# Adding a partial product into the residual ahead of its eviction, in a fused attention and MLP kernel on one Trainium2 core

## The chip, the core and the metric

The kernel runs on one core of a Trainium2 chip. The metric is the device time of one launch in microseconds (us). The core has a matrix engine (TensorE, PE in the profile; its weight loads are PEld), a vector engine (VectorE, DVE), an activation engine (ScalarE, ACT), a general engine (GpSimd, POOL) and a queue engine that issues transfers (SyncE, SP). Each works through its own instructions in order; between engines, semaphores say when a value is there or a buffer is free. TensorE writes its results to PSUM, whose banks VectorE and ScalarE read; GpSimd works on SBUF.

## The reference

A linear attention with decay, followed by a normalised two-layer MLP with a residual:

```
for b in range(nb):                       # blocks of 64 rows of each sequence
    intra = einsum('bhic,bhjc->bhij', qb, kb) * Dmask
    intra = einsum('bhij,bhjd->bhid', intra, vb)
    inter = einsum('bhid,bhde->bhie', qb * lam_pow, kv_state)
    out[:, :, sl] = intra + inter
    kv_state = lam_block * kv_state + einsum('bhsd,bhse->bhde', kb * rev_pow, vb)
x  = out as [4, 768, 512]
xn = (x - mean) / sqrt(var + 1e-6) * g_ln
result = x + relu(xn @ w_ch1) @ w_ch2     # w_ch1 512 x 2048, w_ch2 2048 x 512
```

q, k and v are 4 x 8 x 768 x 64 in float32; the result is 4 x 768 x 512 in float32.

## The kernel before, in words

The 3,072 rows of the result are worked in twelve units of 256 rows (u = 0 to 11, `NU` is 12). A unit is two tiles of 128 rows, called ab = 0 and ab = 1. For each unit the attention part leaves a tile `x` of 128 partitions x 2 x 512 (the residual; four buffers) and, transposed, the normalised input `xT` of the MLP. The scale of the normalisation, `rstd`, is put on at the very end, one value per row. A group of the MLP is one unit: g = u.

The first MLP layer (`m1`, line 502) runs 64 matmuls per group into eight PSUM tiles `pm`, and ScalarE puts each tile through a ReLU into `hT`. The order of all work is written out by hand (lines 1009 to 1284): `units(n)` issues the next n pieces of the MLP, and between them stand the attention steps of the unit ahead, the stores and the loads. Instructions of each engine run in the order in which these lines issue them.

For groups 0 to 5 the second layer is the plain product (`m2`, line 624). For groups 6 to 11 (`WG = 6`) it is a scheme with seven products in place of eight, by Strassen's method, over the two tiles of rows and the two halves of the 512 output columns. `h_sums` (line 520) forms sums of parts of `hT` on VectorE, and sums of the weights (`wt`) are made once. `m2w` (line 599) issues the products P1, P2, P7, P6, P5, P4, P3 in this order, eight matmuls of 256 columns each, spread over eight pieces of seven matmuls. There are four accumulators `pr["a"]` to `pr["d"]` (pwa to pwd in the profile), each 128 x 256 in a bank of its own:

- a takes P1, and then P6 on top of it
- b takes P2
- c takes P7, and then P4 on top of it
- d takes P5, and is then begun anew with P3

All four come from the ring of four `mm` tiles that `pm` uses too, so each has to be read before the ring comes round to it.

As soon as a product is complete, `evict` (line 550) reads it out. `scaled` (line 557) is one VectorE operation: accumulator x rstd + a third operand. `o` is the output tile, 128 x 2 x 512, and `oq[ab][z]` its quarters of 256 columns, as `xq` are those of x. Before the change, an eviction does the following:

- P1: ScalarE reads a x rstd into `ev_u1` (line 569), GpSimd adds x and writes the first quarter (570)
- P2: VectorE adds b into the first quarter
- P7: ScalarE reads c x rstd into `ev_p7` (577)
- P6: VectorE makes quarter (0, 1) from a and x (579)
- P5: VectorE adds d into `ev_p7` (581), makes both quarters of tile 1 from a and x in one operation of 512 columns (582), and GpSimd adds `ev_p7` into quarter (1, 1) (584)
- P4: VectorE adds c into quarter (1, 0) (586)
- P3: VectorE adds d into quarter (0, 1) (591)

The second product in a bank can only begin once the first has been read where its value is needed alone: P6 after ScalarE's read of P1, P4 after ScalarE's read of P7, P3 after VectorE's read of P5.

A group's output is stored by `store(u)` (line 671), two transfers on SP's queue, issued later in the hand-written order. The last group (u = 11) is stored from within `evict` instead: quarter (0, 0) after P2 (line 575, two transfers on SP), all of tile 1 after P4 (line 589, one transfer on SP and one on ScalarE's queue), and quarter (0, 1) after P3 (line 594, one on each).

Of the kernel before, what the change touches and what calls it, by code (L numbers as in the profile page):

```python
# [11 lines left out]
ALU = mybir.AluOpType  # L12
# [5 lines left out]
def kernel(  # L18
# [11 lines left out]
    nc = tc.nc  # L30
# [4 lines left out]
    NU = B * S // W  # L35
    DM = H * D
# [20 lines left out]
    half = [slice(0, 64), slice(64, 128)]  # L57
# [434 lines left out]
    o_of = {}  # L492
    m2s = {}

    def mlp(g):
# [36 lines left out]
        pr = {}  # L532
# [15 lines left out]
        ev = {}  # L548

        def evict(i):  # L550
            u = g
            x, rstd = x_keep[u]
            w = DM // 2
            r = [rstd[:, ab:ab + 1] for ab in range(2)]
            xq = [[x[:, ab, z * w:(z + 1) * w] for z in range(2)] for ab in range(2)]

            def scaled(out, in0, ab, in1):
                nc.vector.scalar_tensor_tensor(out, in0=in0, scalar=r[ab], in1=in1, op0=ALU.mult, op1=ALU.add)  # L558

            def tmp(name):  # L560
                ev[name] = wk.tile([128, w], F32, tag="ev_" + name, bufs=1, name="ev_" + name)
                return ev[name]

            if i == "P1":
                o_of[u] = wk.tile([128, 2, DM], F32, tag="o", bufs=2, name="o")
            o = o_of[u]
            oq = [[o[:, ab, z * w:(z + 1) * w] for z in range(2)] for ab in range(2)]
            if i == "P1":
                nc.scalar.activation(tmp("u1"), pr["a"], ACT.Identity, scale=r[0])  # L569
                nc.gpsimd.tensor_tensor(oq[0][0], ev["u1"], xq[0][0], op=ALU.add)  # L570
            elif i == "P2":
                scaled(oq[0][0], pr["b"], 0, oq[0][0])
                if u == NU - 1:
                    for j in range(2):
                        nc.sync.dma_start(rows_of(u)[j][:, 0, 0:w], o[half[j], 0, 0:w])
            elif i == "P7":
                nc.scalar.activation(tmp("p7"), pr["c"], ACT.Identity, scale=r[1])
            elif i == "P6":
                scaled(oq[0][1], pr["a"], 0, xq[0][1])
            elif i == "P5":  # L580
                scaled(ev["p7"], pr["d"], 1, ev["p7"])
                scaled(o[:, 1].rearrange("p (z w) -> p z w", z=2), pr["a"][:, None, :].to_broadcast([128, 2, w]), 1,
                       x[:, 1].rearrange("p (z w) -> p z w", z=2))
                nc.gpsimd.tensor_tensor(oq[1][1], ev["p7"], oq[1][1], op=ALU.add)  # L584
            elif i == "P4":
                scaled(oq[1][0], pr["c"], 1, oq[1][0])
                if u == NU - 1:
                    for j in range(2):
                        (nc.sync, nc.scalar)[j].dma_start(rows_of(u)[j][:, 1], o[half[j], 1])
            elif i == "P3":  # L590
                scaled(oq[0][1], pr["d"], 0, oq[0][1])
                for j in range(2):
                    if u == NU - 1:
                        (nc.sync, nc.scalar)[j].dma_start(rows_of(u)[j][:, 0, w:], o[half[j], 0, w:])

        products = (("P1", "a", True), ("P2", "b", True), ("P7", "c", True), ("P6", "a", False),
                    ("P5", "d", True), ("P4", "c", False), ("P3", "d", False))
# [1 line left out]
        def m2w(n):  # L599
            lo, hi = 7 * n, 7 * n + 7  # L600
            for q, (i, bank, first) in enumerate(products):
                part = [r for r in range(8) if lo <= 8 * q + r < hi]
                if part:
                    product(i, bank, part, first and part[0] == 0)
                    if part[-1] == 7:
                        evict(i)
# [44 lines left out]
    def rows_of(u):  # L651

        cc, b = divmod(u, B)
        order = "(c p j) d -> j p c d" if u < LB else "(j c p) d -> j p c d"
        return out[b, cc * W:(cc + 1) * W, :].rearrange(order, c=2, j=2)
# [658 lines left out]
```

## Time and profile before

| what | value |
|---|---|
| median of 6 runs | 214.7 us (213.0 to 216.69) |
| the profiled execution | 213.78 us |
| its span, first to last instruction | 212.1 us |
| granted TensorE clock, mean | 0.999 |
| GpSimd's add of P7 (line 584), six times | 726 ns each |
| ScalarE's read of P7 (line 577), six times | 476 ns each |
| VectorE's evictions of 256 columns, of 512 columns | 471 to 484 ns, 743 ns |

The profile is of one execution. The span is shorter than the execution's own time, since it runs from the first to the last instruction only. A row of the timeline has the start in us from the span's start, the duration in us, the engine, the line and the operation, with what it writes and what it reads, and in brackets how long the engine was idle before it and what ended that idle time. A row of the waits has the waiting engine and line, what it waited for, the total in us, how often, and the longest. SPq and ACTq are the queues on which a transfer is issued; such a row is the time of the issue, not of the transfer. Matmuls overlap: a row of eight matmuls begins with the first one and ends with the last, and the next product's row begins before that.

### The profile page before, as it was taken

The page shows a single profiled execution, that of the slowest core. Times are in us where ns is not written, and L with a number is a line of the kernel's source. Part 1 is how long each engine was busy: PE and PEld are TensorE (multiplying, and loading weights), DVE is VectorE, ACT ScalarE, POOL GpSimd, SP SyncE. Part 2 cuts the span into 40 slices and gives each one's busy share as a digit, 9 for nine tenths or more (in the row PEclk, how much of TensorE's full clock was granted, in tenths as well). Part 3 has the DMA queues.
Part 4 walks back from the last instruction along what each step waited for, and adds up shares of the span by engine and source line. Part 5 has one row for each costly group of instructions (what it writes and reads, how often), then busy time and mean ns, then how long its engine had stood idle before and what let it go on. Part 6 is the DMA issues. An engine that isn't in the chain of part 4 may idle for free.

```text
span 212.1 us, 7030 instructions
## 1 busy us (share of the span) xinstructions
PE 199.3 (94%) x3027; PEld 150.8 (71%) x3027; DVE 141.2 (67%) x292; ACT 97.8 (46%) x195; POOL 83.1 (39%) x113
## 2 busy tenths in 40 slices
PE   1989999999999999999999899999999999999991
PEld 0379788544784675685586488888888888988880
DVE  2587570559268437737986589798897887875271
ACT  2854869220452244355093085285383471652620
POOL 4559138239565181228073064182381302011011
PEclk9999999999999999999999999999999999999999
DMA  3999999999999999899899999999995330520312
GB/s 92 295 275 217 188 295 188 203 303 268 221 305 221 195 223 200 175 238 140 162 216 204 138 241 197 203 212 182 208 195 100 82 73 0 124 29 8 94 25 74
DMA packets 94144, 37.15 MB, mean 175 GB/s; under 512 B 68385, under 2 KB 91169, under 8 KB 94114
## 3 DMA queue, kind: packets, MB, share of 16 engines
q1 hardware_dynamic: 89584, 32.32, 70.3%
q0 software_dynamic: 4224, 4.19, 12.6%
q8 instruction: 23, 0.38, 0.8%
q10 hardware_dynamic: 306, 0.20, 0.3%
q14 instruction: 7, 0.06, 0.1%
HBM read 27.27 MB, written 6.29 MB: 158 GB/s over the span
## 4 chain that ended last, share of the span: by engine, by line
PE 75%; DVE 7%; DMA 6%; ACT 4%; POOL 3%; issue 2%; SPq 1%; ACTq 0%; DVEq 0%
PE pm L510 35%; PE pm L641 10%; PE pwa L545 5%; PE pwd L545 5%; PE pwc L545 5%; DMA kqT<-kq 4%; PE pwb L545 2%; PE pm1t L615 2%; PE po L418 2%; DMA g_one<-in_moe_g_ln_dram 2%; PE tp L249 2%; PE po L431 2%; PE sc L272 2%; DVE xc L460 1%; POOL kq L235 1%
## 5 line engine op out<-in xcount | busy, mean ns | idle before, releaser
L510 PE MATMUL pm<-xT,w 128*128 128x256 bf16 x736 | 85.4, 273 | 0.4 <-issue 0.3
L510 PEld LDWEIGHTS <-w 128*128 128x128 bf16 x736 | 69.9, 98 | 10.6 <-issue 1.3
L513 ACT ACTIVATE hT<-pm 128x512 f16<-128x512 f32 x92 | 55.1, 603 | 41.1 <-PE pm L510 40.3
L641 PE MATMUL pm<-w,hT 128*128 128x512 f16 x192 | 43.3, 379 | 0.0
L641 PEld LDWEIGHTS <-hT 128*128 128x128 f16 x192 | 18.2, 98 | 20.6
L312 POOL TENSOR_TENSOR Sn<-Stmp,lam_s 128x256 bf16<-128x256 f32 x16 | 9.8, 613 | 47.5 <-DVE Stmp L390 26.7
L545 PEld LDWEIGHTS <-hs 128*128 128x128 f16 x192 | 18.8, 98 | 2.2
L460 DVE SCALAR_TENSOR_TENSOR xc<-po,mv,g_row 128x512 bf16<-128x512 f32 (+1 forms) x24 | 16.8, 706 | 1.8
L282 DVE TENSOR_TENSOR mA<-sc,keep 128x512 bf16<-128x512 f32 x20 | 13.1, 685 | 7.2 <-PE sc L272 7.1
L453 ACT COPY x<-po 128x512 f32<-128x512 f32 x18 | 9.9, 590 | 16.8 <-PE po L431 10.7
L570 POOL TENSOR_TENSOR o<-ev_u,x 128x256 f32<-128x256 f32 x6 | 4.6, 771 | 30.7 <-ACT ev_u L569 30.7
L545 PEld LDWEIGHTS <-hT 128*128 128x128 f16 x144 | 13.6, 98 | 2.7 <-ACT hT L513 1.2
L455 DVE BATCH_NORM_STATS2 stats<-x 128x6 f32<-128x512 f32 x18 | 12.4, 688 | 3.8 <-ACT x L453 3.8
L528 DVE TENSOR_TENSOR hs<-hT 128x1024 f16<-128x1024 f16 x12 | 9.6, 801 | 7.1 <-ACT hT L513 7.1
L665 DVE SCALAR_TENSOR_TENSOR o<-pm,rstd,x 128x512 f32<-128x512 f32 x12 | 8.8, 744 | 6.9 <-PE pm L641 6.8
L235 POOL TENSOR_TENSOR kq<-qin,lam_q 128x512 bf16<-128x512 f32 x10 | 10.3, 1045 | 6.3 <-DMA qin<-in_q_dram 3.8
L241 POOL TENSOR_TENSOR vb<-vin,lam_p 128x1024 bf16<-128x1024 f32 x6 | 11.4, 1896 | 3.5 <-DMA vin<-in_v_dram 3.5
L235 POOL TENSOR_TENSOR kq<-qin,lam_p 128x512 bf16<-128x512 f32 x12 | 12.3, 1042 | 0.4 <-DMA qin<-in_q_dram 0.4
L241 POOL TENSOR_TENSOR vb<-vin,lam_v 128x1024 bf16<-128x1024 f32 (+1 forms) x7 | 11.6, 1661 | 2.2 <-DMA vin<-in_v_dram 1.1
L584 POOL TENSOR_TENSOR o<-ev_p,o 128x256 f32<-128x256 f32 x6 | 4.4, 726 | 20.5 <-DVE o L558 20.5
L358 DVE TENSOR_TENSOR mA<-sc,keep 128x512 bf16<-128x512 f32 x12 | 8.2, 683 | 2.0 <-PE sc L352 2.0
L558 DVE SCALAR_TENSOR_TENSOR o<-pwa,rstd,x 128x256 f32<-128x256 f32 (+1 forms) x12 | 7.4, 613 | 3.0 <-PE pwa L545 3.0
(124 smaller groups left out, 260.1 us busy)
## 6 DMA issues: line engine op xcount, KB each, us to landing
out_dram<-o SPq DMA_DIRECT2D x22, 256.0 KB, 4.3
w<-in_moe_w_ch_dram POOLq DMA_DIRECT2D x8, 512.0 KB, 8.7
kin<-in_k_dram SPq DMA_DIRECT2D x14, 256.0 KB, 4.1
qin<-in_q_dram SPq DMA_DIRECT2D x14, 256.0 KB, 4.7
vin<-in_v_dram SPq DMA_DIRECT2D x14, 256.0 KB, 5.5
kin<-in_k_dram SPq DMA_DIRECT2D x5, 512.0 KB, 6.8
qin<-in_q_dram SPq DMA_DIRECT2D x5, 512.0 KB, 8.7
vin<-in_v_dram SPq DMA_DIRECT2D x5, 512.0 KB, 8.2
```

The source lines that it names most:

```text
L235: eng.tensor_tensor(part(1, st[u]["kq"], ALL)[:, :, :, j], src[:, :, :, j], lq[:, :, :, None].to_broadcast([128, NP, 2, D]), op=ALU.mult)
L241: eng.tensor_tensor(st[u]["vb"][:, hs], qkv_in[u]["v"][:, hs], lv.to_broadcast([128, n, 2, D]), op=ALU.mult)
L282: nc.vector.tensor_tensor(s[f"mA{hf}"][:, e], s[f"sc{hf}"][e], kp[:, None, :, :].to_broadcast([128, 2, 2, 128]), op=ALU.mult)
L312: eng.tensor_tensor(dst, src, lam_s[:, :, None].to_broadcast([128, NP, D]), op=ALU.mult)
L453: nc.scalar.copy(x, po)
L455: nc.vector.bn_stats(stats, po if early else x)
L460: nc.vector.scalar_tensor_tensor(xc[:, sl], in0=po[:, sl], scalar=mv[:, 0:1], in1=g_row[:, sl], op0=ALU.subtract, op1=ALU.mult)
L510: nc.tensor.matmul(pm[:, b, :], lhsT=w1[n // W2K][:, kk, (n % W2K) * 128:(n % W2K + 1) * 128], rhs=xT_of[g][:, kk, 0:N], start=(b == 0 and ...
L513: nc.scalar.activation(hT[:, u * NB:(u + 1) * NB, 0:N], pm, ACT.Relu)
L528: nc.vector.tensor_tensor(s13, b[:, :, 1:2, :].to_broadcast([128, n, 2, 128]), b[:, :, 0:4:3, :], op=ALU.subtract)
L545: nc.tensor.matmul(pr[bank], lhsT=lhs(r), rhs=rhs, start=(first and r == 0), stop=(r == KB // 2 - 1), skip_group_check=True)
L641: nc.tensor.matmul(acc[i], lhsT=hT[:, kk, i * 128:(i + 1) * 128], rhs=w2[kk // W2K][:, kk % W2K, :], start=(kk == 0), stop=(kk == KB - 1))
```

## The change

At P7, GpSimd adds ScalarE's read-out into x itself (quarter (1, 1) of x), at once. P6's eviction makes both quarters of tile 1 from a and x, in one operation of 512 columns; x already has P7 in it there. P5's eviction adds d into quarter (1, 1) of the output and then makes quarter (0, 1) from a and x. GpSimd's add after P5 goes. In the last group the quarters of tile 1 are stored one by one, each as it becomes complete (after P5 and after P4), through a helper that issues one transfer on SP's queue and one on ScalarE's.

```diff
             elif i == "P7":
                 nc.scalar.activation(tmp("p7"), pr["c"], ACT.Identity, scale=r[1])
+                nc.gpsimd.tensor_tensor(xq[1][1], ev["p7"], xq[1][1], op=ALU.add)
             elif i == "P6":
-                scaled(oq[0][1], pr["a"], 0, xq[0][1])
-            elif i == "P5":
-                scaled(ev["p7"], pr["d"], 1, ev["p7"])
                 scaled(o[:, 1].rearrange("p (z w) -> p z w", z=2), pr["a"][:, None, :].to_broadcast([128, 2, w]), 1,
                        x[:, 1].rearrange("p (z w) -> p z w", z=2))
-                nc.gpsimd.tensor_tensor(oq[1][1], ev["p7"], oq[1][1], op=ALU.add)
+            elif i == "P5":
+                scaled(oq[1][1], pr["d"], 1, oq[1][1])
+                scaled(oq[0][1], pr["a"], 0, xq[0][1])
+                last_rows(1, 1)
             elif i == "P4":
                 scaled(oq[1][0], pr["c"], 1, oq[1][0])
-                if u == NU - 1:
-                    for j in range(2):
-                        (nc.sync, nc.scalar)[j].dma_start(rows_of(u)[j][:, 1], o[half[j], 1])
+                last_rows(1, 0)
             elif i == "P3":
                 scaled(oq[0][1], pr["d"], 0, oq[0][1])
-                for j in range(2):
-                    if u == NU - 1:
-                        (nc.sync, nc.scalar)[j].dma_start(rows_of(u)[j][:, 0, w:], o[half[j], 0, w:])
+                last_rows(0, 1)
+
+        def last_rows(ab, z):
+            u = g
+            if u < NU - 1:
+                return
+            sl = slice(z * (DM // 2), (z + 1) * (DM // 2))
+            for j, eng in enumerate((nc.sync, nc.scalar)):
+                eng.dma_start(rows_of(u)[j][:, ab, sl], o_of[u][half[j], ab, sl])
```

## The prediction

> **What bounds the kernel now.** I read four views: the page's totals, the waits of TensorE from 122 us on (where the groups with seven products run), the timeline of one such group, and the timeline of the end.
>
> ```profile
> PE 199.3 (94%) x3027; PEld 150.8 (71%) x3027; DVE 141.2 (67%) x292; ACT 97.8 (46%) x195; POOL 83.1 (39%) x113
> PEclk9999999999999999999999999999999999999999
> ```
>
> ```profile
> PE sc L352 <- DMA kqT<-kq: 1.0, 1, 1.0
> PE pm L510 <- issue: 0.3, 1, 0.3
> ```
>
> These two are all of TensorE's waits from 122 to 206 us, the DMA one at 122 us, before the first product (129.5 us). From there TensorE is never idle and at full clock. Idle time put in front of it is added to the end; work taken off another engine gains nothing. Now the third of the six groups (start, duration, engine, line):
>
> ```profile
> 161.16 1.04 PE L545 MATMUL pwc<-wt,hs 128*128 128x256 f16 x8
> 162.03 1.04 PE L545 MATMUL pwa<-wt,hs 128*128 128x256 f16 x8
> 162.29 0.48 ACT L577 ACTIVATE ev_p<-pwc,rstd 128x256 f32<-128x256 f32 x1 [1.27 <-PE pwc L545]
> 162.91 1.04 PE L545 MATMUL pwd<-wt,hs 128*128 128x256 f16 x8
> 163.11 0.48 DVE L558 SCALAR_TENSOR_TENSOR o<-pwa,rstd,x 128x256 f32<-128x256 f32 x1 [0.55 <-PE pwa L545]
> 163.78 1.04 PE L545 MATMUL pwc<-wt,hT 128*128 128x256 f16 x8
> 164.05 0.48 DVE L558 SCALAR_TENSOR_TENSOR ev_p<-pwd,rstd,ev_p 128x256 f32<-128x256 f32 x1 [0.46 <-PE pwd L545]
> 164.45 0.74 DVE L558 SCALAR_TENSOR_TENSOR o<-pwa,rstd,x 128x512 f32<-128x512 f32 x1
> 164.65 1.04 PE L545 MATMUL pwd<-w,hs 128*128 128x256 f16 x8
> 165.27 0.72 POOL L584 TENSOR_TENSOR o<-ev_p,o 128x256 f32<-128x256 f32 x1 [3.39 <-DVE o L558]
> 165.30 0.48 DVE L558 SCALAR_TENSOR_TENSOR o<-pwc,rstd,o 128x256 f32<-128x256 f32 x1
> ```
>
> TensorE begins a product every 0.87 us: P7 at 161.16, P6 162.03, P5 162.91, P4 163.78, P3 164.65. P3 overwrites bank d, so it must wait until P5's value there is read. That read (DVE, 164.05) ends at 164.53, 0.12 us before P3. This is the narrowest place. VectorE idles 0.55 us before P6's eviction and 0.46 us before P5's.
>
> **What doesn't change.** Per group VectorE keeps six operations and 1,792 columns (before 256+256+256+512+256+256, after 256+512+256+256+256+256), ScalarE its two reads, GpSimd two adds. "P5's eviction is one operation" frees bank d no earlier: d's read was already the first of P5's two operations. The removed add L584 (0.73 us) released nobody on TensorE: the stores of groups 6 to 10 wait for P3's eviction, which ends later (166.21 against 165.99). Gain there: nothing. Bank a, read last by P5's second operation in both kernels, is wanted after P3 only.
>
> **What is added: GpSimd in the chain to P3.** P6's eviction, now 512 wide, reads the quarter of x that GpSimd just wrote; P5's eviction reads what P6's wrote; VectorE works in order, and P3 waits for it. GpSimd is free: L570 ended at 161.88. From the end of P7's read, 162.29 + 0.476 = 162.77:
> - to GpSimd's start 0.085 (P1's read ended 161.015, L570 began 161.10);
> - the add 0.726 (L584; L570, with the same kind of operands, took 726 to 788 ns, the upper value where a VectorE operation with two SBUF operands was already running, which is not so here);
> - to VectorE 0.06: the Smid that follows a GpSimd Sn started 0.04 after its end (168.11, 168.15), and this operation waits for two engines, as P5's eviction does, which began 0.10 after its last matmul (163.95, 164.05), so 0.04 to 0.10;
> - the 512-wide operation 0.743, from PSUM, as in L558's long form;
> - to the dependent operation 0.11: P4's eviction at 165.30 began so long after the 512-wide one ended (165.19), with the same two waits (own engine and TensorE); other dependent VectorE pairs show 0.03 to 0.04;
> - P5's read of d 0.484;
> - to TensorE 0.06: the first transpose of xc began 0.05 after its VectorE operation (29.60, 29.65).
>
> Sum 2.27 us. Today's schedule gives from that read's end to P3 164.65 − 162.77 = 1.88 us. TensorE therefore stands 2.27 − 1.88 = 0.39 us before P3. In the first group the read ends at 132.92 and P3 begins at 134.85: 1.93, stall 0.34; the other five have 1.88 or 1.89. With every link at its lower value (0.08, 0.72, 0.04, 0.74, 0.03, 0.47, 0.05 = 2.13) the stall is 0.25, with every upper one (0.09, 0.79, 0.10, 0.75, 0.11, 0.49, 0.06 = 2.39) 0.51.
>
> Behind the waiting P6 operation VectorE has only P5's, P4's and P3's evictions; P4's begins no later than now. Behind the stalled P3 on TensorE lies all later work, and nothing there waits for anything else that could swallow the delay. The 0.1 us between P3's last matmul and the next 64x64 matmul recurs at changes of matmul shape all through the kernel, so I don't count it as cover.
>
> Two rules bear on this. The Trainium skill, VectorE: DVE Perf Modes, section on the TRN2 errata, prices an operation from PSUM at 120 cycles plus its columns at 0.96 GHz: 658 and 392 ns, 1.05 us for the pair. The rows say 0.743 + 0.484 = 1.23. With the page's prices the stall is 0.21 us, with the rows' 0.39. I take the rows. And Perfetto Trace Analysis, "Optimizing Scalar/DVE Operations", says that larger operations pay where the engine is saturated, but where it is not and holds others up, smaller ones let work finish sooner. VectorE is at 67%: the rule speaks against putting the wide operation ahead of the one TensorE waits for. As two halves, the one without GpSimd first, the chain would hold 0.484 in place of 0.743 and the stall would be 0.13. The change doesn't do that.
>
> **The end.** In the last group:
>
> ```profile
> 207.41 0.48 DVE L558 SCALAR_TENSOR_TENSOR o<-pwd,rstd,o 128x256 f32<-128x256 f32 x1
> 207.71 0.47 SPq L589 DMA_DIRECT2D out_dram<-o  x1
> 207.71 0.54 ACTq L589 DMA_DIRECT2D out_dram<-o  x1
> 208.27 0.55 SPq L594 DMA_DIRECT2D out_dram<-o  x1
> 208.35 0.75 ACTq L594 DMA_DIRECT2D out_dram<-o  x1
> ```
>
> The second half of o waits for GpSimd's add (206.96 + 0.72 = 207.68) and is issued at 207.71; P3's quarter, ready at 207.89, queues behind that issue until 208.27 and 208.35. It lands 2.3 and 2.5 us later, at 210.85 at the latest; the span ends 1.25 after that. Changed, still without the earlier groups' delay: P5's read ends at 206.28 + 0.39 = 206.67, its stores go at 206.7; P4's eviction ends near 207.47, its stores take the queues from 207.5 to 208.05; P3's eviction is at 207.41 + 0.39 = 207.80, done 208.28, stores at 208.32. So the queueing that goes pays for the last stall: the last issue is where it was, with 64 KB instead of 128 KB per queue just ahead. Landing after 2.0 us (this group's first 64 KB stores, alone) to 2.5: a gain of 0 to 0.5, I take 0.3. The two added issues, one on each queue, fit into gaps.
>
> **Sum.** Five earlier groups 0.34 + 4 × 0.39 = 1.90, less 0.3: +1.6 us. The profiled execution took 213.78 (span 212.1 and 1.7 around it): 215.4. The median of the runs is 214.7: 216.3, which I predict. The bounds give 5 × 0.25 − 0.5 = +0.75 and 5 × 0.51 = +2.55.
>
> **Rivals.**
> - *The stall at P3*, as above: 216.3, 75%. For it: 0.12 us of room against an operation that starts 0.5 us later and is 0.26 longer. Own range 215.3 to 217.4.
> - *The chain fits* (the side not slower): if it takes under 1.88 us, P3 doesn't wait and only the end moves: P3's quarter, ready at 207.89, would be issued behind P4's at 208.1 and land 0.2 earlier by that and up to 0.5 by the smaller load, −0.5 in all: 214.2. It decides below 1.88, which needs 0.39 us off my sum; even the lower values total 2.13. A stall of 0.1 gives 5 × 0.1 − 0.3 = +0.2, 214.9. Together 16%.
> - *The chain is longer*, GpSimd's add slowed and each hand-over at its upper value: 5 × 0.51 = +2.55, 217.25, 7%.
> - *Faster by over 0.5%*: there is no idle TensorE time to recover and the end offers 0.7 us at most, 0.3%. Only scatter: 2%.
>
> Half a per cent, 1.1 us, is about what a measurement of this kernel can tell from no change. Of the main case some 2 points fall below it, so slower is 0.80, same 0.18, faster 0.02. The range 214.4 to 218.0 takes in the bounds and the scatter of the median (runs from 213.0 to 216.69).
>
> **What would show it.** P6's eviction waiting for GpSimd's x and starting 0.5 us later; P3's first matmul 2.2 to 2.3 us after the end of P7's read; a new TensorE wait on VectorE, some 0.4 us, six times; the last stores issued with nothing queued before them, landing in under 2.5. P2's stores and the order of all operations stay as they are. Wrong if P3 follows P4 without a gap, or if TensorE's later waits shrink by as much.

## The result and the profile after

The changed kernel takes 216.66 us (median of 33 runs) against 214.59 us for the kernel before (70 runs on the same chips): ratio 1.0106, interval 1.0087 to 1.0125, slower by 1.9 to 2.7 us. The ratios leave out executions more than 1.5% above the fastest of their kernel (the profiles of e1 and e6 below are such, so their first starts are not used), a limit that one fast run moves; over all runs the two means are 1.8 us apart. Later runs of it gave 1.0085 (1.0052 to 1.0118) and 1.0123 (1.0086 to 1.0160). The kernel before, run against itself, gave 0.9969 (0.9939 to 0.9999) and 0.9971 (0.9931 to 1.0011): a single comparison can be off by 0.3%. The forecast was 216.3.

The profiled execution took 216.43, its span 214.73 (212.06 before). The totals of the page, busy us of each engine:

```profile
PE 200.7 (93%) x3027; PEld 150.7 (70%) x3027; DVE 140.0 (65%) x292; ACT 98.2 (46%) x195; POOL 83.8 (39%) x113
PEclk9999999999999999999999999999999999999999
```

As many matmuls, at the same clock. The totals do not say where the time went: TensorE's busy time grew by 1.4 of the 2.7 us by which the span grew, since the ends of its matmuls are modelled and part of a short wait counts as work. TensorE's waits from 122 us to the end:

```profile
PE pm L510 <- issue: 1.2, 2, 0.9
PE pwd L545 <- DVE o L558: 0.9, 5, 0.2
PE sc L352 <- DMA kqT<-kq: 0.2, 1, 0.2
```

The middle line is new: P3 waits for VectorE's eviction. (Waits under some size aren't listed, here the first of the six, and the view counts from the modelled end of the matmuls before, so the starts of the products measure the wait better.) And among VectorE's waits in the same stretch:

```profile
DVE o L558 <- POOL x L578: 5.6, 6, 1.1
```

That is P6's eviction waiting for GpSimd's add, six times. The third group's timeline, which answers to the one shown of before:

```profile
163.37 1.04 PE L545 MATMUL pwc<-wt,hs 128*128 128x256 f16 x8
164.50 0.48 ACT L577 ACTIVATE ev_p<-pwc,rstd 128x256 f32<-128x256 f32 x1 [1.27 <-PE pwc L545]
165.05 0.72 POOL L578 TENSOR_TENSOR x<-ev_p,x 128x256 f32<-128x256 f32 x1 [0.97 <-ACT ev_p L577]
165.11 1.04 PE L545 MATMUL pwd<-wt,hs 128*128 128x256 f16 x8
165.81 0.75 DVE L558 SCALAR_TENSOR_TENSOR o<-pwa,rstd,x 128x512 f32<-128x512 f32 x1 [1.05 <-POOL x L578]
165.99 1.04 PE L545 MATMUL pwc<-wt,hT 128*128 128x256 f16 x8
166.67 0.48 DVE L558 SCALAR_TENSOR_TENSOR o<-pwd,rstd,o 128x256 f32<-128x256 f32 x1
167.07 0.48 DVE L558 SCALAR_TENSOR_TENSOR o<-pwa,rstd,x 128x256 f32<-128x256 f32 x1
167.20 1.03 PE L545 MATMUL pwd<-w,hs 128*128 128x256 f16 x8 [0.18 <-DVE o L558]
```

Read it along the diagonal: ScalarE's read of P7 ends at 164.98, GpSimd 165.05 to 165.77, the wide eviction 165.81 to 166.56, the read of bank d 166.67 to 167.15, P3 at 167.20. P3 begins 1.21 us after P4 (165.99), where before it was 0.87: 0.34 us lost on TensorE. The end of the last group:

```profile
207.50 1.14 SPq L575 DMA_DIRECT2D out_dram<-o  x2
209.89 2.08 SPq L599 DMA_DIRECT2D out_dram<-o  x3
209.90 2.18 ACTq L599 DMA_DIRECT2D out_dram<-o  x3
210.99 0.48 DVE L558 SCALAR_TENSOR_TENSOR o<-pwd,rstd,o 128x256 f32<-128x256 f32 x1 [0.34 <-PE pwd L545]
```

The three stores of each queue begin at 209.9, and the last of them at 211.50; 3.23 us later the span ends (214.73). Before it was 3.71 us from the last issue (208.35) to the end (212.06). The 64 KB stores on ScalarE's queue, first before, then after, with the median time from issue to landing last:

```profile
out_dram<-o ACTq DMA_DIRECT2D x1, 64.0 KB, 2.5
out_dram<-o ACTq DMA_DIRECT2D x3, 64.0 KB, 2.2
```

Since TensorE sets the pace, the starts of P1 in the six groups (6 to 11) measure the stages. All profiles of this study, in us, from the traces to 0.001 us and then rounded ("P3 − P4" is the distance of the first matmuls, first group / others; 0.87 is no stall):

| kernel | first P1 at | 6 to 7 | 7 to 8 | 8 to 9 | 9 to 10 | 10 to 11 | last P1 to end | P3 − P4 |
|---|---|---|---|---|---|---|---|---|
| before | 129.51 | 15.01 | 14.79 | 14.54 | 13.95 | 13.20 | 11.05 | 0.87 / 0.87 |
| before, second (e7) | 127.94 | 15.04 | 14.54 | 14.54 | 13.94 | 13.20 | 11.05 | 0.87 / 0.87 |
| before, third (e10) | 129.28 | 15.29 | 14.77 | 14.54 | 13.95 | 13.20 | 11.05 | 0.87 / 0.87 |
| after | 130.25 | 15.93 | 15.33 | 14.88 | 14.29 | 13.54 | 10.50 | 1.16 / 1.22 |
| after, second (e8) | 131.21 | 15.43 | 15.01 | 14.88 | 14.28 | 13.54 | 10.50 | 1.16 / 1.22 |
| after, third (e11) | 130.03 | 15.88 | 15.32 | 14.87 | 14.28 | 13.54 | 10.50 | 1.16 / 1.22 |
| e1, new in the last group only | 132.50 | 15.46 | 14.54 | 14.54 | 13.94 | 13.20 | 10.50 | 0.87; last 1.22 |
| e2, new in the other five only | 131.14 | 15.97 | 15.06 | 14.88 | 14.28 | 13.53 | 11.06 | 1.16 / 1.22; last 0.87 |
| e3, P7 added by VectorE | 131.87 | 15.61 | 15.02 | 15.00 | 13.95 | 13.20 | 10.15 | 1.01 / 0.87; third 1.07 |
| e4, GpSimd twice | 130.59 | 15.76 | 15.34 | 15.34 | 14.74 | 14.00 | 10.97 | 1.62 / 1.68 |
| e5, wide eviction in halves | 129.59 | 15.80 | 14.80 | 14.62 | 14.02 | 13.28 | 10.26 | 0.89 / 0.95 |
| e6, bank d first | 131.70 | 15.68 | 14.60 | 14.54 | 13.94 | 13.20 | 10.29 | 0.87 / 0.87 |
| e6 again (e12) | 129.37 | 15.54 | 14.86 | 14.54 | 13.95 | 13.20 | 10.32 | 0.87 / 0.87 |
| e9, smaller stores only | 130.74 | 15.04 | 14.82 | 14.54 | 13.95 | 13.20 | 11.05 | 0.87 / 0.87 |

The three columns from 8 to 11 and the end repeat to 0.01 us. There the change costs 0.34 us per group, as much as the distance of P3 from P4 grew (1.215 − 0.873): nothing later takes the stall back. Five stalls are 0.29 + 4 × 0.345 = 1.67 us; the last stage, its own stall included, is 0.55 shorter. Together +1.12 us. The median grew by 2.1, the mean over all runs by 1.8. The rest is spoken of below.

### The profile page after: what moved, and what is told of

It reads as the page before. It is cut to its first block, busy times and chain, and to the rows that moved or that the text cites. A ratio compares the mean times of both kernels' runs of the same rounds, so it can differ in the third digit from the quotient of the medians.

```text
span 214.7 us, 7043 instructions
## 1 busy us (share of the span) xinstructions
PE 200.7 (93%) x3027; PEld 150.7 (70%) x3027; DVE 140.0 (65%) x292; ACT 98.2 (46%) x195; POOL 83.8 (39%) x113
## 4 chain that ended last, share of the span: by engine, by line
PE 46%; DMA 17%; issue 15%; DVE 8%; POOL 6%; SPq 5%; ACT 1%; POOLq 0%; DVEq 0%; ACTq 0%
PE pm L510 27%; DMA vin<-in_v_dram 6%; PE pm L646 5%; DMA qin<-in_q_dram 4%; DMA kqT<-kq 4%; SPq L75 3%; DVE o L558 3%; PE pwd L545 2%; DMA xT<-xc 2%; PE pwa L545 2%; POOL x L578 2%; POOL vb L241 1%; DVE xc L460 1%; PE po L431 1%; POOL kq L235 1%
## 5 line engine op out<-in xcount | busy, mean ns | idle before, releaser
L528 DVE TENSOR_TENSOR hs<-hT 128x1024 f16<-128x1024 f16 x12 | 9.1, 754 | 7.6 <-ACT hT L513 7.6
L241 POOL TENSOR_TENSOR vb<-vin,lam_v 128x1024 bf16<-128x1024 f32 (+1 forms) x7 | 11.8, 1693 | 4.3 <-DMA vin<-in_v_dram 4.3
L241 POOL TENSOR_TENSOR vb<-vin,lam_p 128x1024 bf16<-128x1024 f32 x6 | 11.8, 1973 | 2.3 <-DMA vin<-in_v_dram 2.3
L558 DVE SCALAR_TENSOR_TENSOR o<-pwa,rstd,x 128x512 f32<-128x512 f32 (+1 forms) x12 | 7.4, 613 | 5.6 <-POOL x L578 5.6
L442 ACT COPY seen<-po 128x8 f32<-128x8 f32 x8 | 1.0, 168 | 18.5 <-PE po L431 18.5
```

The lines of the kernel that those rows point to most:

```text
L241: eng.tensor_tensor(st[u]["vb"][:, hs], qkv_in[u]["v"][:, hs], lv.to_broadcast([128, n, 2, D]), op=ALU.mult)
```

## The experiments

Theory A: the chain ScalarE, GpSimd, VectorE, VectorE delays P3, and the end gains. Theory B: about 1 us of the 2 comes from elsewhere in the change.

**e1: the new evictions and stores in the last group only**; of each branch of `evict` both forms are kept, as here for P6 (against the kernel before; the other branches are left out).

```diff
-            elif i == "P6":
+            elif u == NU - 1 and i == "P6":
+                scaled(o[:, 1].rearrange("p (z w) -> p z w", z=2), pr["a"][:, None, :].to_broadcast([128, 2, w]), 1,
+                       x[:, 1].rearrange("p (z w) -> p z w", z=2))
+            elif not (u == NU - 1) and i == "P6":
                 scaled(oq[0][1], pr["a"], 0, xq[0][1])
```

> The new evictions and stores in the last group only, groups 6 to 10 as before. If the chain through GpSimd is the cost (theory A): P3 stalls 0.34 us once, and the end is shorter than before's by what the changed trace showed there (from P1 of the last group to the end 11.1 before, 10.47 after): 0.3 to 0.6 us faster than before. If the time above what the stalls explain (theory B: about 1 us of the 2 us, tied to the new stores or to something not seen) sits in the end, this run is slower than before by 0.5 to 1 us.

Ratio to before 0.9958 (0.9921 to 0.9996). The end is 10.50 against 11.05, with the stall of P3 (0.35) inside it. As A has it; the end is no place for a hidden cost.

**e2: the new evictions in groups 6 to 10 only**, the last group as before; the same two forms, with the other condition.

```diff
-            elif i == "P6":
+            elif u < NU - 1 and i == "P6":
...
+            elif not (u < NU - 1) and i == "P6":
```

> The new evictions in groups 6 to 10 only; the last group and its stores as before. Theory A: five stalls of 0.29 to 0.35 us, +1.7 us against before, and the end as before (11.1 us from the last group's P1). Theory B, a further cost in these groups beyond the stall at P3: +2.3 to +2.8.

Ratio 1.0141 (1.0059 to 1.0222), of six runs: it lies above both theories, and its interval holds both +1.7 us (1.008) and +2.8 (1.013), so the times don't decide. The stages do in part: five stalls of the size seen in the changed kernel, three later stages longer by 0.33 to 0.34 each, the end 11.06. The first two stages hold more (table). Effects of e1 and e2 in the trace are separate and add up.

**e3: P7 added into x by VectorE, straight from bank c** (from here to e6, edits are against the changed kernel).

```diff
-                nc.scalar.activation(tmp("p7"), pr["c"], ACT.Identity, scale=r[1])
-                nc.gpsimd.tensor_tensor(xq[1][1], ev["p7"], xq[1][1], op=ALU.add)
+                scaled(xq[1][1], pr["c"], 1, xq[1][1])
```

> As the changed kernel, but P7 is added into x by one VectorE operation straight from bank c; ScalarE's read and GpSimd's add of P7 are gone, everything else is kept. Theory A: P6's wide operation starts about 0.05 us after its matmuls, d is read in time, P3 follows P4 without a gap in all six groups; 0.3 to 0.7 us faster than before, some 2.4 us faster than the changed kernel. If the wide operation or the order of P5's reads is the cost and not the hand-over through GpSimd, P3 still stalls some 0.3 us and the time stays near the changed kernel's 216.6.

Ratio 1.0008 (0.9973 to 1.0042), near the kernel before and some 1% under the changed one; by its end (−0.91), its first stall (+0.13) and its third stage (+0.46) it should be 0.3 us under before, which the interval admits. That no group would have a gap was wrong: groups 7, 9, 10 and 11 have none, but the first and third stall by 0.13 and 0.20. The third group:

```profile
160.37 1.90 POOL L241 TENSOR_TENSOR vb<-vin,lam_p 128x1024 bf16<-128x1024 f32 x1 [1.10 <-DMA vin<-in_v_dram]
160.58 2.23 DVE L528 TENSOR_TENSOR hs<-hT 128x1024 f16<-128x1024 f16 x1
164.28 0.73 POOL L570 TENSOR_TENSOR o<-ev_u,x 128x256 f32<-128x256 f32 x1 [2.02 <-ACT ev_u L569]
164.43 0.86 DVE L529 TENSOR_TENSOR hs<-hs,hT 128x512 f16<-128x512 f16 x1
166.06 0.48 DVE L558 SCALAR_TENSOR_TENSOR x<-pwc,rstd,x 128x256 f32<-128x256 f32 x1
166.64 0.75 DVE L558 SCALAR_TENSOR_TENSOR o<-pwa,rstd,x 128x512 f32<-128x512 f32 x1
167.49 0.48 DVE L558 SCALAR_TENSOR_TENSOR o<-pwd,rstd,o 128x256 f32<-128x256 f32 x1
168.03 1.03 PE L545 MATMUL pwd<-w,hs 128*128 128x256 f16 x8
```

VectorE came late to this group. A sum of hidden values (L528) took 2.23 us beside GpSimd's scaling of v (L241, 160.37 to 162.27); in the changed kernel it took 1.08 there, with less of L241 beside it. So VectorE came out of it 0.3 us after P1's start (162.50), where in the changed kernel it is 0.8 us before. From 160.58 to the read of d it has no pause that the timeline shows, and with seven evictions a group instead of six it didn't catch up: d is read at 167.97, P3 begins at 168.03. (The 0.86 us of L529 is no delay of its own: in the changed kernel it is the next sum, L530, that takes 0.83 beside GpSimd's add of P1.) Another 0.24 us of the third stage is lost later, at an attention matmul (L431, 170.18). GpSimd's hand-over is the cause of the steady 0.34, but taking it out puts its work on the engine next in the chain.

**e4: one more GpSimd operation in the chain.**

```diff
+                nc.gpsimd.tensor_copy(ev["p7"], ev["p7"])
                 nc.gpsimd.tensor_tensor(xq[1][1], ev["p7"], xq[1][1], op=ALU.add)
```

> As the changed kernel, with one more GpSimd operation of 128x256 (a copy of P7's read-out onto itself) ahead of the add, so that the chain is longer by one GpSimd operation, 0.4 us by the casts of the same size. Theory A: every P3 stalls 0.4 us longer, 0.75 in place of 0.34: six times 0.4, 2.4 us slower than the changed kernel. If the chain has room, or P3 waits for something else, under 0.5 us slower.

Ratio to before 1.0239 (1.0154 to 1.0324), 1.3% or 2.8 us above the changed kernel's 1.0106. In the trace every P3 begins 1.68 us after P4 (first group 1.62), 0.46 later than in the changed kernel, and every steady stage is 0.46 longer, six times 0.46 being 2.8 us:

```profile
165.20 0.40 POOL L578 COPY ev_p<-ev_p 128x256 f32<-128x256 f32 x1 [0.95 <-ACT ev_p L577]
165.68 0.72 POOL L579 TENSOR_TENSOR x<-ev_p,x 128x256 f32<-128x256 f32 x1
166.44 0.75 DVE L558 SCALAR_TENSOR_TENSOR o<-pwa,rstd,x 128x512 f32<-128x512 f32 x1 [1.51 <-POOL x L579]
```

0.40 for the copy and 0.08 for the hand-over to the add. What is put into the chain comes out at the end of each group, 0.46 of 0.48: it has no room left.

**e5: the wide eviction as two of 256 columns**, the half that needs nothing of GpSimd first.

```diff
-                scaled(o[:, 1].rearrange("p (z w) -> p z w", z=2), pr["a"][:, None, :].to_broadcast([128, 2, w]), 1,
-                       x[:, 1].rearrange("p (z w) -> p z w", z=2))
+                scaled(oq[1][0], pr["a"], 1, xq[1][0])
+                scaled(oq[1][1], pr["a"], 1, xq[1][1])
```

> As the changed kernel, but P6's wide eviction is two operations of 256 columns, first the half of tile 1 that needs nothing of GpSimd, then the half that does. Theory A, with the changed trace's own hand-overs: the second half can start at GpSimd's end + 0.04, lasts 0.48 in place of 0.75, so that P3 stalls 0.07 to 0.10 us per group in place of 0.34; 1.4 us faster than the changed kernel over the groups before the last. If the width of the operation doesn't matter (GpSimd's wait alone is the cost, or the larger number of VectorE operations is paid too), the stall stays at 0.3 or more.

Ratio 1.0037 (0.9995 to 1.0079). The third group:

```profile
163.72 0.73 POOL L578 TENSOR_TENSOR x<-ev_p,x 128x256 f32<-128x256 f32 x1 [0.85 <-ACT ev_p L577]
164.65 1.04 PE L545 MATMUL pwc<-wt,hT 128*128 128x256 f16 x8
165.07 0.48 DVE L558 SCALAR_TENSOR_TENSOR o<-pwd,rstd,o 128x256 f32<-128x256 f32 x1
165.60 1.03 PE L545 MATMUL pwd<-w,hs 128*128 128x256 f16 x8
```

P3 stalls 0.08 us in place of 0.34 (first group 0.02), and stages 8 to 11 are 0.07 to 0.08 longer than before: the half that waits is 0.27 us shorter than the whole, and the stall shrank by that. One operation more on VectorE cost nothing in these stages. So of the 0.34 us, 0.27 are the width of the operation behind the wait. By its stages (stalls +0.34, end −0.79) this kernel should be 0.45 us faster than before; the comparison has it 0.8 us slower, with an interval from −0.1 to +1.7 us, and leaves that open.

**e6, and again e12: bank d read first, into x.**

```diff
             elif i == "P6":
-                scaled(o[:, 1].rearrange("p (z w) -> p z w", z=2), pr["a"][:, None, :].to_broadcast([128, 2, w]), 1,
-                       x[:, 1].rearrange("p (z w) -> p z w", z=2))
+                scaled(oq[1][0], pr["a"], 1, xq[1][0])
+                scaled(oq[0][1], pr["a"], 0, xq[0][1])
             elif i == "P5":
-                scaled(oq[1][1], pr["d"], 1, oq[1][1])
-                scaled(oq[0][1], pr["a"], 0, xq[0][1])
+                scaled(xq[1][1], pr["d"], 1, xq[1][1])
+                scaled(oq[1][1], pr["a"], 1, xq[1][1])
```

> GpSimd's add of P7 into x stays where the change put it, but P5's first operation, the one that P3 waits for, reads bank d and x only (x + P7 + d into x), and the quarter of tile 1 is made from it and a afterwards; P6's eviction needs nothing of GpSimd. Theory A: GpSimd's value is ready at about 0.85 us after P7's read, before P5's eviction needs it, so P3 never waits: stages as before, and the end shorter by 0.5 to 0.9 us; 0.3 to 0.9 us faster than before, 2 to 2.7 faster than the changed kernel. If the use of GpSimd there, by itself, costs time, it stays within 0.5 us of the changed kernel.

> The version with bank d read first, once more against before. By its stages it should be 0.86 us faster than before (end 10.24 in place of 11.1, no stall), a ratio of 0.996; with the resolution shown by the kernel before against itself, 0.992 to 1.000.

Ratios to before 0.9972 (0.9938 to 1.0005) and 0.9924 (0.9893 to 0.9955). GpSimd does just what it does in the changed kernel, yet no P3 waits (e12, third group):

```profile
163.30 0.72 POOL L578 TENSOR_TENSOR x<-ev_p,x 128x256 f32<-128x256 f32 x1 [0.97 <-ACT ev_p L577]
163.56 0.88 DVE L558 SCALAR_TENSOR_TENSOR o<-pwa,rstd,x 128x256 f32<-128x256 f32 x2 [0.56 <-PE pwa L545]
164.23 1.04 PE L545 MATMUL pwc<-wt,hT 128*128 128x256 f16 x8
164.50 0.48 DVE L558 SCALAR_TENSOR_TENSOR x<-pwd,rstd,x 128x256 f32<-128x256 f32 x1
165.10 1.04 PE L545 MATMUL pwd<-w,hs 128*128 128x256 f16 x8
```

GpSimd ends at 164.02, beside VectorE's two operations for P6; the read of d needs its value only at 164.50. P3 comes 0.87 us after P4. Stages 8 to 11 are those of before, and the end is shorter by 0.76 and 0.74 us (10.29 and 10.32; the 0.86 expected came from a span rounded to 0.1 us): 0.35% is what the stages explain. Against the changed kernel this version clearly gains. Against before, the shorter end is shown and the gain in time is likely, but not shown: the second interval lies below 1, the first just reaches it, but an interval wholly below 1 came out for the kernel before against itself too (0.9939 to 0.9999), and over all runs the means are equal in the first comparison and 1.0 us apart in the second.

**e9: only the smaller stores**, with the evictions as before (against the kernel before).

```diff
-                        (nc.sync, nc.scalar)[j].dma_start(rows_of(u)[j][:, 1], o[half[j], 1])
+                        for z in range(2):
+                            sl = slice(z * w, (z + 1) * w)
+                            (nc.sync, nc.scalar)[j].dma_start(rows_of(u)[j][:, 1, sl], o[half[j], 1, sl])
```

> The evictions as before in all groups; in the last group the two quarters of tile 1 are stored by a transfer each, both after P4. If the shorter end comes from the smaller transfers by themselves, the end is 10.5 us from the last group's first product as in the changed kernel, 0.6 us faster than before. If it comes from the third quarter being complete 0.9 us earlier (the new evictions), the end stays at 11.0 to 11.5 us: two issues of 0.5 us each stand ahead of P3's quarter, and the time is that of before or 0.2 us more.

Ratio 1.0008 (0.9959 to 1.0058), end 11.05, as before.

```profile
208.78 1.11 SPq L591 DMA_DIRECT2D out_dram<-o  x2
208.79 1.38 ACTq L591 DMA_DIRECT2D out_dram<-o  x2
209.98 0.55 SPq L596 DMA_DIRECT2D out_dram<-o  x1
210.26 0.56 ACTq L596 DMA_DIRECT2D out_dram<-o  x1
```

The last issue (210.26) is 3.08 us before the end of the span (213.34), 0.63 us less than before's 3.71; but P3's quarter, ready at 209.18, had to stand behind two issues on ScalarE's queue until 210.26. That is 7.97 us after the last P1, 0.62 later than before (208.35 − 201.00 = 7.35), and eats the whole gain. Smaller transfers at the end do land sooner; they pay only because the new evictions have a quarter complete earlier, so that its issue is over by then.

**e7, e10 and e8, e11: before and after, unchanged, again.**

> The kernel before, unchanged, as a second profile and for the resolution of the comparison. Stages from the first product on as in the first profile (15.0, 14.8, 14.5, 13.95, 13.2 us between the first products of neighbouring groups, 11.1 to the end). Theory A with scatter in the part before the first product: that part differs from 129.5 us by 1 us or more although nothing is changed. If instead the changed kernel has a true cost in the first part, this one starts its first product near 129.5 again.

> The kernel before, for the part ahead of the first product, which took 129.5 and 127.9 us here and 129.6 to 132.5 in eight profiles of other kernels whose instructions there are the same. If that part only scatters (theory A), this one starts its first product anywhere from 127.5 to 132.5. If the kernels other than before have a true cost there (theory B), it starts at 127.5 to 129.5 again. Stages afterwards as in the two earlier profiles.

> The changed kernel once more. Theory A: P3's first matmul 1.16 us after P4's in the first group and 1.22 in the others, 10.5 us from the last group's first product to the end, both to 0.02 us as in the first profile; the first product's start differs by up to 2 us. Ratio to before 1.005 to 1.013. Theory B (a further cost of about 1 us inside the stages): the stages after the second one again add up to more than the stalls.

> The changed kernel, for the same question. Theory A: first product anywhere from 127.5 to 132.5 us. Theory B: 130 to 132. P3 1.16 and 1.22 us after P4, end 10.45 us, as before.

Stages 8 to 11, the end and P3 − P4 repeat to 0.01 us, as A has it. The parts ahead do not. The first product began at 127.9 to 129.5 in the three profiles of before, at 130.0 to 131.2 in those of the changed kernel, and at 129.4 to 131.9 in the rest, e9 with before's evictions (130.74) and e12 (129.37) among them. The instructions up to there are the same. But the profiled executions of before were quick ones, 0.8, 2.7 and 0.9 us under the medians of their runs, and those of the changed kernel lie within 0.3 us of theirs. Their first starts are 1.6 us apart on average; if an execution's distance from its median arises ahead of the first product, some 0.3 us of that is left (an estimate from these numbers).

And TensorE's waits from 120 us on show a wait "issue" (the view names nothing that ended it) in the first layer after group 6. The second profile of before:

```profile
PE pm L510 <- issue: 0.3, 1, 0.3
```

It is 0.3, 0.3 and 0.5 us with before, 1.2, 0.4 and 1.2 after, 0.3 with e9, 0.3 with e4, and 0.8 to 1.1 in the others (of the 1.2, 0.3 is a second such wait, after group 7). With the stalls taken off, the first two stages take 29.81 us on average before (29.80, 29.58, 30.05) and 30.34 after (30.63, 29.81, 30.57). The page of the kernel before has a line that bears on it:

```profile
q8 instruction: 23, 0.38, 0.8%
```

These are 23 packets of 16 KB, loads of instructions. In all fourteen profiles the wait, and the second one where there is one, ends 1.2 to 1.7 us after such a packet has ended: before, the packet ran from 136.52 to 137.94 and TensorE went on at 139.39; in the changed kernel it ran from 138.30 to 139.37 and TensorE went on at 141.04. And the long waits are those with the late packets: counted from P1, with the stall at P3 taken off, the packet ends at 8.4 to 8.7 us where the wait after group 6 is 0.3 to 0.5 us, and at 8.6 to 9.2 where it is 0.8 to 1.0. So most likely TensorE waits there for its next instructions; no run tests it, and why the packet comes later in some profiles is not shown. It takes no new evictions: e1, whose group 6 is that of before, has 0.8 us.

## Why the prediction was right, and where its terms were off

- **TensorE without slack, so a stall goes to the end one for one.** Right: 0.34 us longer in each of the three steady stages, and e4's 0.46 as well.
- **The chain, 2.27 us.** Measured in the third group 2.22: 0.07 to GpSimd (0.085), 0.72 (0.726), 0.04 to VectorE (0.06), 0.75 (0.743), 0.11 (0.11), 0.48 (0.484), 0.05 to TensorE (0.06). The stall was forecast at 0.39 and 0.34 in the first group; it is 0.345 and 0.29. Three of the hand-overs were put a little too high. Five groups: 1.67 in place of 1.90.
- **The page's prices against the rows** (the Trainium skill, VectorE: DVE Perf Modes, section on the TRN2 errata). In the chain, the 256 and 512 columns took 0.484 and 0.75 us, not the 0.392 and 0.658 estimated from the page. From the start of one eviction to the start of an independent one behind it are 0.40 us (166.67, 167.07), which is near the page's price; but what P3 waits for is the end.
- **The rule on smaller operations** (the Trainium skill, Perfetto Trace Analysis, "Optimizing Scalar/DVE Operations") holds here: for two halves the prediction had a stall of 0.13; e5 shows 0.08.
- **The end.** The mis-sized term: forecast −0.3 from a range of 0 to 0.5, measured −0.55. The last issue came about as forecast, 7.27 us after the last P1 (211.50 − 204.23; forecast 208.32 − 201.00 = 7.32; before 7.35). The last store on ScalarE's queue landed 2.20 us after its issue in place of 2.55, near the 0.3 that I had taken off. The rest is behind the landing: from there to the end of the span it was 1.16 us before (I had put it at 1.25) and 1.03 after, where I had expected no change.
- **What was hidden** stayed hidden: bank a, the removed add, GpSimd's queue, VectorE's order.
- **The sum.** The terms I named came to +1.6; measured they are +1.12 (1.67 − 0.55). The median grew by 2.1 us, the mean by 1.8. So the nearness of 216.3 to 216.66 is in part luck: it rests on something I hadn't in the sum. I wrote that TensorE is never idle from the first product on, though the line above that sentence shows 0.3 us of "issue", at 139.4 us. This wait was longer by about 0.5 us in the profiles of the changed kernel. What is then left, 0.2 to 0.5 us, is less than a single comparison can be off by (0.3%, 0.6 us). That the change makes the wait longer is not shown: three profiles a side don't settle its mean, and kernels with the evictions of before in that group (e1), with hardly a stall (e5) or with none (e6, e12) have a long one as well. Theory B stays open for this half microsecond; more profiles of both kernels would be needed. What is shown is that the stalls at P3 exist, that they come from GpSimd's place ahead of the wide eviction, and that with P3 free (e6, e12) the kernel isn't slower than before.

## What to carry to other kernels

Before moving work ahead to shorten a later step, find the one read that the bound engine waits for, and add up the chain that ends in it, hand-overs included; here 0.12 us of room met half a microsecond. A value from a slower engine may come early or late, as long as it enters behind that read, or where the read comes anyway (e6): the same GpSimd add cost 0.34 us a group in one place and nothing in another. And where an operation must wait for another engine, keep it narrow: put what doesn't depend on the wait into an operation of its own ahead of it.

## What the runs showed of the hardware that was not expected

- The same instructions up to the first product took from 127.9 to 131.9 us in twelve profiles, while the stages from group 8 on repeat to 0.01 us where the evictions are the same. A change of 1 us is read from such stages, not from one span.
- A wait of TensorE of 0.3 to 1.0 us that no engine ends recurs in the first layer after group 6, in all fourteen profiles, 1.3 to 1.7 us behind the end of a 16 KB load of instructions: most likely TensorE was out of instructions.
- An operation of VectorE can take longer beside one of GpSimd: in groups 7 and 8 of every profile the sum L528 took 1.1 to 2.2 us where it ran beside GpSimd's scaling of v (L241); at 163.72 in e3, clear of that, it took 0.67.
- At the end of the kernel, cutting the 128 KB transfers just ahead of the last ones to 64 KB (the last ones had that size already) brought the end 0.5 to 0.6 us closer to the last issue (3.23 and 3.08 against 3.71 us).
